# Another stored order of instructions and twenty warm-up matmuls instead of fourteen, in a one-core transformer block

## The chip, the core and the metric

The kernel runs on one core of a Trainium2 chip. A core has five engines that run their own instruction streams side by side: TensorE (PE in the profile; its weight loads are PEld), VectorE (DVE), ScalarE (ACT), GpSimd (POOL) and SyncE (SP, which here only starts transfers). They meet through semaphores. The metric is the device time of one execution in microseconds (us); lower is better.

## The reference

One sequence of 2048 positions with 448 features goes through two halves, each under adaptive layer norm. The six modulation vectors come from `mod = silu(c) @ w_mod`.

```python
h = layernorm(x) * (1 + ca) + sa
q, k, v = split(h @ wqkv)                 # 16 heads of 28
scores = q @ k.T * 28 ** -0.5             # masked: 0 <= i - j < 256
x = x + ga * (softmax(scores) @ v @ wo)
h = layernorm(x) * (1 + cb) + sb
z = gelu(h @ w_in)                        # 1792 wide, halves z1 and z2
g = w_sp @ layernorm(z2) + b_sp[:, None]  # w_sp is 2048 x 2048
x = x + gb * ((z1 * g) @ w_out)
```

Inputs and output are bf16.

## The kernel before

The sequence is cut into 16 tiles of 128 positions, in blocks of 1, 1, 2, 4, 4 and 4 tiles. For a block the kernel computes the statistics of x (st, L609; mv_all, L612), the reciprocal deviation (rs_all on POOL, L617), the normalised tile xn (L631 on DVE, L630 on POOL, or ScalarE), its transpose hT (by PE against an identity for the first three blocks, evacuated at L693 on ScalarE or L698 on VectorE; by transfers for the rest, modulated at L707), and then the projections to Q, K and V. Heads lie in groups of four; the weights of Q and K are therefore copied from the loaded wqk_raw into a padded layout WQK (L733 to L735, on DVE, ScalarE or POOL). The first tile's projections read wqk_raw itself where they can, four 32-column matmuls side by side (`mm_heads`, L779).

Attention goes by single tiles at first and then by pairs: scores into PSUM (28-row matmuls on QKT), exp on ScalarE into the tile arena (L887), causal and window masks on POOL (L890), products with V (32-column matmuls on Vaug), then on VectorE a 32x32 transpose oq out of PSUM (L1058), reciprocal (L1059), normalisation o_sb (L1063) and transpose back (L1067), and the projection wo with the residual added into x_sb (L1077). The second half computes z1 and z2 by blocks, and a last phase (from about 116 us on) multiplies w_sp, transposed by transfers, with the normalised z2 and projects out.

Nothing is scheduled while the kernel is built. Each step is recorded as a numbered operation with its dependencies and its choices of engine (`Planner.op`, L66), and a stored string `ORDER` (L179) names the operations in the order in which they are emitted: a number, behind a point the choice of engine, behind a slash the PSUM bank or buffer. `schedule` (L82) reads it; `emit` (L117) splits it into one in-order program for each engine and puts a semaphore wait ahead of an instruction where an operand, or the last user of its buffer, demands one:

```python
for tok in ORDER.split():
    head, _, picks = tok.partition("/")
    num, _, opt = head.partition(".")
    o = self.ops[int(num)]
```

So the string decides three things at once: what stands behind what on an engine, on which engine an operation with a choice runs, and which buffer's last reader it has to wait for. An engine never overtakes a waiting instruction. `column_tiles` (L106) then looks at PE's row: 128-row matmuls that stand between column-tiled ones are issued as four 32-column pieces as well (L464 instead of L467).

The first operations on PE are warm-ups: matmuls of a constant tile warm that nothing reads (loop at L1243). They stand in `ORDER` like everything else and can be put between waits.

Of the kernel before, what the change touches and what calls it, by code (L numbers as in the profile page):

```python
# [179 lines left out]
32 34 1 0 22 21 25 23 27 1693/0 1694 1695 1696 1697 1698 2 3 4 8 11 31 67 68 36 6 7 5 35 69 37/7 1699 12 24 28 26 70 71/4 9 10 20 13 15 18 14 74/6  # L180
72/2 33 38 39 40/1 41 42 43 44 45 46 47 76/7 48 49 50 78/4 51 52 53 54 55 56 73.1 125 126 75 79 1700 1701 127 90/6 95/1 85/0 62.2 63.2 1702 105/2 1703
96 86 91 80/4 106 81 180 128 129 130.1/1 77 57.1 60.1 61.1 65.1 64.1 87 97 182 92 82 88 98 83 93 84 99 94 181 89.1 183 66 58.2 59.2 184 185 115/3 116
117 107 118 108 119 109 131/7 132.1 245 249 133/4 134 1704 1705 496/0,0 498/1 150/0 1706 135/2 140/1 151 152 165/3 166 141 136 137 138 153 167 168 142
143 139 169 246 186 251 247 250 252 248 154 144 110/1 100/0 101 111 170/2 171 112 145/3 113 172 114 173 102 103 104 174.1 160/1 155/0 146 147 148 149
156 157 161 158 159 162 163 164 497/1,1 30.1 188.1/2 190/3 120/6 253 17 413 501/0 187.1/4 189 191.1 254 255 256/3 192/1 193 194 121 175/2 176 513/0,1
517/7 514/5 177 122 123 494/3 124.1 215/1 178 216 179 225/0 227 217 226 228 502 499 16 495 19 260 257.1/1 261 229 520/1,0 523/8 521/9 218.1 195/2
219.1 196 230/0 231 197 198 233 232 220/3 221 199.1 205/1 207 206 208 200/2 201 203 202 223 222 209 534/1,0 234.1 417 334 328 330 332 331 204 224
536/1 535/5 258.1/2 262 259.1/4 518 515 29 263 235/1 210/2 240/3 241 238.1 213.1 243.1 212 237 242 244.1 500/0 211 214.1 267 537/1,0 329 335 333 336
503 236 504/0 264.2 538 540 323/3 278/2 266.1 326 281 324 279 265.1 325 327 337 414 505 411 338 239.1 539 280 282 524/0 506/1 342/3 339/2 340/1 341/4
343 345 346 344 542/0,1 543/1 546/0 544/4 541 547/2 545 548 268/3 271 519 270 516 288/2 290 522 303/1 269 304 272 525/0 549/1,0 550/0 551/4 289 305  # L190
308/3 273/0 291.1 306.1 311.1 276.1 412 415 526 292.1 418 307.1 416 527/0 274 275 277 309 552/1,0 553 554 555 556 310 312.1 283/2 285 558/0 284 298/1
528/2 419 420 300 557 299 560 286.1 301.1 287 587/0,1 588/3 589/2 561 559 293/3 562 507/0 302.1 294 295 296 569/0 570 508/1 529/2 509 510 297 530 511
512 590/1,0 591 531 532 563/0 567 565 566 564 571.1/0 572/0 573/1 574 533 349 568 578/0 593 595/2,1 599/4 348.1 347.1 350 421 575 576 376/0 378 577
579 377 379 380.1 580/0 592 594 596/0 597/1 602/1,0 603/4 604/5 361/1 364 362 363 365.1 581/1 908 911 905 906 910 907 381/0 382 384 605/1,2 1426 606
383 385.1 608 366/1 367 368 369 370.1 614/0 611 610 640/1,0 642/0 641/1 598 600/2 613 422.2/3 936 938 582/1 583 584 585 586 937 942 607 318/3 320 609
601 356/2 357 358 396/1 612 615 622/0 623 943 399.1 359.1 321.1 360 643/1,0 646 398 319 397 322.1 922/0 923 924 925 926 400.1 927 928 929 930 644
648/2,0 649/3 313/1 315 314 619/0 316 652/2 617 620 655/1,2 657/2 939 940 941 944 616 317.1 621 618 423.1/0 425.1/1 424.1/2 624.1/0 647 645 625/1 913
912 426 909 428 631/0 656/4 351/1 352 354.1 353 406/2 409 371/3 386/0 658/1,0 661 632 633/0 374.1 389.1 388 634/0 355.1 407 408 410.1 635/1 636 387
390.1 945 659 372 637 638 639 693/0,1 373 375.1 653/4 650/1 651 654 662 668/0 666 667 664 663 660 665 946 675/0 401/1 404.1 427 429 431.2 430.1 432.1
695/5 694/3 676 947.1/0 433.1 696/1,2 697 698 403 402 626/0 405.1 627 628 629 630 701/0,1 677/0 454/1 457 674/0 456 455 458.1 672 671 673 669 670  # L200
684/0 961 962 678/0 699 705/0 700 953/2 706/1 707 702/2 703/4 708/1,2 709/1 710/0 391/1 393 392 449/0 450 452 451 453.1 685 686/1 711/1,0 712 713 714
715 394 395.1 687/1 464/3 467 679/0 680 466 681 682 444/2 465 468 446 746/0,1 447 445 683 918 1425 917 948 748/4 448.1 704 949/0 951/1 723/0 722 726
727 725 724 737/0 738 739.1/0 747/2 434/1 749/1,2 435 437 436 438.1 752 753 688/0 689 690 691 692 959 963 964 965 750 751 754/0,2 755/3 721/0 720 718
719 459/1 461 761/1,0 460 756/0 757 758/1 759/2 760 960 966 462 463.1 967 762/0 763/5 479/3 469/2 480 717 716 728/0 729 482.1 472.1 481 470 483
764/1,0 765 730/1 471 473.1 439/1 484/0 767 731/0 950 1428 952 954 921 1429 485 487 486 968 488.1 969 740/1 799/2,1 800/3 442.1 441 440 443.1 773/0
766 768 958.1 956.1 770 769 772 771 774 781/0 782 955 976.1/2 801/1 802/0,2 805 806 741/1 742 743 732/0 733 734 735 736 783/1 803 804 807/2,1 811/4
744 776/0 775 777 778 779 812/3 814/1,0 745 784/0 780 808/2 816/4 809/0 813 785/1 786 787 788 815/0 790/0 791 789 792/0 474/0 817/0,2 818 477 475 476
478.1 931/1 793/2 919 920 977 916 915 933 932 810 819 820 821 852/0,1 853/2 854/5 822/0 826 823 825 957.1 794/3 795 796 824 1035/2 1036 827 834/0 797
798 1037 935 934 986 835 988 982 984 983 989 985 987 1038 1043.1 855/0,1 856 858 970/1 974/2 972/0 857 859 1052/0 1054 1039/2 1040 1069/3 1071 1070
1053 1041 1072 1055 1042 1077.1 1060.1 1044.1 860/0,1 864/1 1090/1 1056/3 1091 828/0 832 830 831 489/2 829 833 1058 1057 1092 490 1435 914 1434 971  # L210
973 975 836.1/1 843/0 990 865/2 991 861/3 862/4 1059 492.1 1093 1061.1 867/1,0 869/0 868/4 1073/0 491 837/0 838/3 839 840 841 1095 493.1 844 845.1/0
980.2 1075 1086/1 1088 1087 842 1005 1076 1089 1094 846/1 992 981 978.1 997.1/1 979.1 999/2 870/2,0 873 998 1000 1431 995.1/0 866 863 874 871 872
1096/1 1295/7 1296 1305/6 1297 1307 1300/3 1150/0 1301 1154 1156 1074 1078 847/2 848 1151 849 1152 1330/1 1303 1298 1079/0 1299 1157 1153 1333 1308
850 851 1155 1306 876/0 878 1332 1302 1304 1103/2 1104 880 1331 1334 993/1 1335/7 875 879 1336 1107/1 877 1108 1340/1 1081 1007 1080 887/0 1006 1082
1008 888 1342 1105 1106 1110 1338 1343 1309 1158/2 1009 1160 1097 889.1/0 890/1 885/0 886 1124/0 882 1315/6 1109 1111.1 1112.1 883 1120 1337 881 884
896/0 1316 1122 1317 1339 1310/3 1320/7 1312 1341 1344 1325/0 1126 1322 1323 1318 1313 1328 1127 1123 1321 1121 996 994 1010 1011 1319 1012.1/2 891/3
1324 1014.1/1 1444 1436 1015 1013 1445 1430 1446 1449 892 1125 893 1128/3 897 1001.1 898.1/0 1003.2 899/0 894 900/0 1326 1370/6 1311 1180/0 1375/7 901
902 903 1184 1002.1 1004.1 1377 1186 1185 1181 1327 1159 1161 1162 895 1098 1099 1100 1163 1329 1314 904 1365/2 1290/1 1366 1368 1373 1378 1293 1183
1187 1022 1164 1023 1101 1102 1020 1021 1083 1024 1129 1025 1084 1026 1130 1029.1/2 1027.1/0 1030 1028 1433 1432 1457 1440 1437 1438 1452 1441 1453
1439 1443 1427 1442 1456 1451 1450 1376 1182 1292 1367 1371 1291 1372 1188/2 1190 1085 1189 1019.1 1369 1374 1294 1379 1285/0 1199/0 1286 1380/3 1200  # L220
1195 1201 1355/2 1197 1381 1357 1169/1 1165 1166 1171 1350/1 1196 1198 1202 1168 1383 1358 1353 1288 1172 1018.1 1191 1131 1045/1 1132 1133 1047 1192
1193 1046 1048 1049 1134 1050 1033.1 1034.1 1203/0 1205 1051 1351 1352 1016.2 1354 1287 1289 1210/0 1211 1170 1167 1382 1212 1356 1173/3 1214 1359
1174 1204 1194 1206 1207 1175 1176 1177 1360/1 1362 1345/0 1361 1229/1 1231 1225 1346 1217 1213 1017.2 1232 1348 1363 1228 1215 1226 1216 1031.2 1384
1364 1218/1 1390/3 1385/1 1230 1227 1233/2 1410/2 1392 1347 1391 1386 1255/0 1256 1259 1139/1 1135 1178 1179 1219 1220 1221 1208 1209 1222 1261 1349
1032.2 1257 1140 1142 1388 1393 1138 1262 1258 1062/3 1063 1223 1064 1234 1065 1224 1260 1387 1400/0 1394 1389 1141 1405/3 1402 1406 1407 1137 1401
# [72 lines left out]
def bass_adaLN_cond__sliding_block__mixer_gmlp__prompt_kernel(  # L298
# [809 lines left out]
    for bi, (T, z2s, z1s) in enumerate(BATCH):  # L1108
        gelus = []
        pr = T + 0.9  # L1110
        for zi, t in enumerate(z2s):
# [3 lines left out]
            def hst(c_, r, t=t):  # L1115
# [3 lines left out]
                           lambda c_, r, i=i: w_in_sb[r, c_, FH + i * D:FH + (i + 1) * D], D, joint=joint, idx=i, rprio=zp + 0.005) for i in range(2)]  # L1119
# [184 lines left out]
```

## Time and profile before

| | us |
|---|---|
| median of 3 runs | 268.02 (267.23 to 268.22) |
| profiled execution | 268.87 |
| its span | 267.1 |
| PE busy | 259.2 |
| VectorE busy | 167.2 |
| ScalarE busy | 128.3 |
| POOL busy | 96.6 |

How the rows are read: a timeline row has the start, the length, the engine, the line, the operation, what it writes and reads, partitions and sizes, how many instructions it joins, and in brackets the idle time ahead of it with what ended that time. A DVE, ACT or POOL instruction can overlap the next by a little. A row of stages has for each engine the busy time and, in brackets, the instructions in it. A releaser is put down by the semaphore event that was last by the profile, and "issue" means that the profile shows no semaphore for which the engine waited.

### The profile page before, as it was taken

What the parts mean: (1) busy time and instruction counts of PE and PEld (TensorE: products, weight loads), DVE (VectorE), ACT (ScalarE), POOL (GpSimd) and SP (SyncE); (2) the same over time, 40 slices, a digit from 0 to 9 for tenths busy, and PEclk for the clock granted to TensorE, in tenths of its full rate; (3) what the DMA queues carried; (4) which work ended last, traced back from release to release, by engine and by line L of the source; (5) the groups of instructions that cost most, each with busy time, mean ns of one, the idle gap of its engine ahead of it and who ended that gap; (6) DMA issues with size and microseconds to landing.
All of it is one profiled execution on the core that took longest, in us unless ns stands there. A gap on an engine that the chain in (4) does not pass through costs nothing.

```text
span 267.1 us, 7649 instructions
## 1 busy us (share of the span) xinstructions
PE 259.2 (97%) x3341; PEld 128.9 (48%) x3341; DVE 167.2 (63%) x388; ACT 128.3 (48%) x182; POOL 96.6 (36%) x148
## 2 busy tenths in 40 slices
PE   7999799999989999999999999999999999999996
PEld 3666345655445554544444444444444444444453
DVE  3899979978879899669988711306111814314455
ACT  4899879989989999866896300000000000000000
POOL 3784747878785888564422300000000000000000
PEclk9999999999999999999999999999999999999999
DMA  6963163574095590857799890000000000001023
GB/s 225 365 174 64 22 158 116 130 125 103 2 106 160 134 132 2 122 120 141 168 183 140 199 189 7 2 0 0 0 2 0 0 0 2 0 17 52 2 86 121
DMA packets 61022, 23.86 MB, mean 89 GB/s; under 512 B 49854, under 2 KB 60861, under 8 KB 60989
## 3 DMA queue, kind: packets, MB, share of 16 engines
q1 hardware_dynamic: 60715, 22.92, 40.5%
q8 instruction: 26, 0.43, 0.7%
q10 hardware_dynamic: 274, 0.46, 0.5%
q14 instruction: 7, 0.06, 0.1%
HBM read 9.47 MB, written 1.84 MB: 42 GB/s over the span
## 4 chain that ended last, share of the span: by engine, by line
PE 92%; DVE 3%; DMA 2%; issue 1%; ACT 0%; SPq 0%; DVEq 0%
PE ps L467 82%; PE ps L464 9%; DMA wmod_sb<-in_w_mod_dram 2%; DVE xn L631 1%; PE ps L779 1%; DVE oq L1058 1%; ACT arena L887 0%; DVE Vaug L837 0%; DVE hT L707 0%; DVE x_sb L1077 0%; DVE o_sb L1063 0%; DVE st_all L609 0%; DVE QKT L820 0%; SPq L498 0%; DVE mv_all L612 0%
## 5 line engine op out<-in xcount | busy, mean ns | idle before, releaser
L887 ACT ACTIVATE arena<-ps 128x1024 bf16<-128x1024 f32 x76 | 72.7, 1030 | 2.5 <-PE ps L467 2.3
L1212 DVE TENSOR_TENSOR tmpg<-ps,bsp_bc 128x512 bf16<-128x512 f32 x28 | 19.1, 688 | 63.6 <-PE ps L467 63.5
L467 PE MATMUL ps<-QKT,z 128*128 128x512 bf16 x224 | 50.1, 379 | 0.0
L890 POOL TENSOR_SCALAR_AFFINE_SELECT arena<-arena 128x512 f32<-128x512 f32 x60 | 40.4, 688 | 17.5 <-ACT arena L887 14.6
L467 PEld LDWEIGHTS ps<-QKT,z 128*128 128x128 bf16 x224 | 21.9, 98 | 26.4 <-ACT z1T L1154 0.3
L617 POOL TENSOR_TENSOR rs_all<-ve_all,neghalf 128x1 f32<-128x1 f32 (+2 forms) x27 | 18.7, 700 | 23.9 <-DVE ve_all L616 23.6
L467 PE MATMUL ps<-w_spD,z 128*128 128x512 bf16 x112 | 26.9, 379 | 0.0
L467 PE MATMUL ps<-w_spC,z 128*128 128x512 bf16 x112 | 26.8, 379 | 0.0
L467 PE MATMUL ps<-w_in_sb,hT 128*128 128x448 bf16 (+1 forms) x108 | 25.9, 354 | 0.0
L467 PE MATMUL ps<-hT,w_in_sb 128*128 128x512 bf16 (+1 forms) x94 | 24.3, 380 | 0.0
L467 PE MATMUL ps<-hT,WQK 128*128 128x128 bf16 (+3 forms) x127 | 21.9, 301 | 1.4 <-DVE mv_all L612 1.4
L467 PE MATMUL ps<-w_out_sb,z1T 128*128 128x448 bf16 (+2 forms) x119 | 22.3, 341 | 0.0
L609 DVE BATCH_NORM_STATS2 st_all<-z2raw 128x6 f32<-128x448 bf16 x32 | 18.9, 615 | 2.1 <-ACT z2raw L1135 1.6
L467 PE MATMUL ps<-arena,Vaug 128*32 128x128 bf16 x720 | 18.5, 221 | 1.3 <-issue 1.2
L609 DVE BATCH_NORM_STATS2 st_all<-x_sb 128x6 f32<-128x448 bf16 x32 | 18.7, 609 | 1.4 <-DMA x_sb<-in_A_x_dram 1.3
L467 PE MATMUL ps<-QKT 28*64 28x64 bf16 (+3 forms) x944 | 17.8, 210 | 0.8 <-issue 0.4
L467 PEld LDWEIGHTS ps<-arena,Vaug 128*32 128x32 bf16 x720 | 14.1, 95 | 8.4 <-issue 1.4
L1154 ACT ACTIVATE z1T<-ps 128x512 bf16<-128x512 f32 x28 | 15.8, 601 | 4.6 <-PE ps L467 2.9
L467 PEld LDWEIGHTS ps<-w_spD,z 128*128 128x128 bf16 x112 | 11.0, 98 | 13.1
L467 PEld LDWEIGHTS ps<-w_spC,z 128*128 128x128 bf16 x112 | 11.0, 98 | 13.1
L467 PEld LDWEIGHTS ps<-QKT 28*128 28x128 bf16 (+1 forms) x944 | 11.3, 98 | 12.2 <-ACT arena L887 7.9
L467 PEld LDWEIGHTS ps<-w_out_sb,z1T 128*128 128x128 bf16 x119 | 11.6, 98 | 10.2
(92 smaller groups left out, 340.5 us busy)
## 6 DMA issues: line engine op xcount, KB each, us to landing
wmod_sb<-in_w_mod_dram SPq DMA_DIRECT2D x8, 224.0 KB, 4.1
w_in_sb<-in_B_w_in_dram SPq DMA_DIRECT2D x8, 224.0 KB, 3.0
out_dram<-fin SPq DMA_DIRECT2D x16, 112.0 KB, 1.7
x_sb<-in_A_x_dram SPq DMA_DIRECT2D x3, 448.0 KB, 6.1
bsp_bc<-in_B_b_sp_dram SPq DMA_DIRECT2D x1, 512.0 KB, 5.3
wqk_raw<-in_A_wqkv_dram SPq DMA_DIRECT2D x1, 452.0 KB, 5.6
wmod_sb<-in_w_mod_dram SPq DMA_DIRECT2D x1, 448.0 KB, 4.3
wmod_sb<-in_w_mod_dram ACTq DMA_DIRECT2D x1, 448.0 KB, 4.8
```

Source lines behind the costliest of these rows:

```text
L464: last = e.matmul(out_[32 * j:32 * j + 32], lhsT=lhsT[:, 32 * j:32 * j + 32], rhs=rhs, start=st, stop=sp, tile_position=(0, 32 * j), **kw)
L467: return e.matmul(out_, lhsT=lhsT, rhs=rhs, start=st, stop=sp, **kw)
L609: st = [dve("%sst%d" % (name, i), prio, dve_ns(D), lambda e, i=i, s_=s_: e.bn_stats(st_all[:, slot, t, i, :], s_()), deps, tens) for i, s_ ...
L617: r = pool(name + "rs", prio, 420 + 148 * n, lambda e: e.tensor_tensor(rs_all[:, slot, t0:t1], ve_all[:, slot, t0:t1], neghalf[:, t0:t1], ...
L631: return e.tensor_scalar(dst, src, mv_all[:, slot, t, 0:1], rs_all[:, slot, t:t + 1], ALU.subtract, ALU.mult)
L779: last = e.matmul(out_[32 * j:32 * j + 32], lhsT=lhsT[j], rhs=rhs, start=st, stop=sp, tile_position=(0, 32 * j))
L887: return P.op(name, pr, [("act", 925, lambda e: e.activation(e_out(), e_in(), ACT.Exp, scale=SCALE))], [s_op, t_exp0], tens + [pt], table= ...
L890: return pool(name, pr, pool_ns(n), lambda e: e.affine_select(out=pt32(slot_out.slot, off, dims), in_=pt32(slot_in.slot, off, dims), patte ...
L1058: tq = dve("oq%d" % j, pr - 10, dve_ns(512), lambda e, pv_ten=pv_ten, qt=qt: e.transpose(out=oq[:, qt.slot, :], in_=ps[:, pv_ten.slot, :]) ...
L1154: g = P.op("z1g%d_%d" % (tb, ft), pr - 19, [("act", act_ns(512), lambda e: e.activation(z1T[:, ft, tb * 512:(tb + 1) * 512], ps[:, ten.slo ...
L1212: a = dve("ga%d_%d" % (tb, ft), pr, dve_ns(512), lambda e, tb=tb, ten=ten, tg=tg: e.tensor_tensor(tmpg[:, tg.slot, :], ps[:, ten.slot, :], ...
```

## The change

Two things change: the loop that records the warm-ups, and the string. All other code is the same, and so is what is computed.

```diff
-    for i in range(14):
-        n_ = 512 if i < 9 else 256
+    for i in range(20):
+        n_ = 512 if i < 10 else 256
```

All 59 lines of the string differ; the first of each is shown.

```diff
 ORDER = """
-32 34 1 0 22 21 25 23 27 1693/0 1694 1695 1696 1697 1698 2 3 4 8 11 31 67 68 36 6 7 5 35 69 37/7 1699 12 24 28 26 70 71/4 9 10 20 13 15 18 14 74/6
+21 1693/0 1694 1695 1696 0 32 35 34 15 1 2 3 4 8 6 7 11 27 22 25 36 37/0 1697 1698 1699 1700 1701 33 38 40/1 41 42 43 44 45 46 47 48 49 50 51 52 53 54
...
```

The new order uses other engines for 53 operations. Warm-ups apart, PE, ScalarE, VectorE and POOL do the same operations as before in sum: ScalarE has 181 instead of 179 of them, VectorE 390 instead of 386, POOL 138 instead of 144. PE has 3404 matmuls instead of 3341, since more of the 128-row ones are cut into column tiles, and 110 changes of the number of rows used by consecutive matmuls (128, 64 or 32) instead of 116.

The start of PE's row, before (c goes through one,crz; modulation through sc_sb,wmod_sb; transposes through ident,xn):

```order
L467 MATMUL ps<-warm 128x512 x6
L467 MATMUL ps<-one,crz 128x1 x4
L467 MATMUL ps<-warm 128x512
L467 MATMUL ps<-ident,xn 128x128 x2
L467 MATMUL ps<-sc_sb,wmod_sb 128x1 x16
L467 MATMUL ps<-ident,xn 128x128
L467 MATMUL ps<-sc_sb,wmod_sb 128x1 x6
L467 MATMUL ps<-ident,xn 128x128
L467 MATMUL ps<-sc_sb,wmod_sb 128x1 x10
L467 MATMUL ps<-warm 128x512 x2
L779 MATMUL ps<-hT,wqk_raw 32x128 x12
```

And now:

```order
L467 MATMUL ps<-warm 128x512 x4
L467 MATMUL ps<-one,crz 128x1 x4
L467 MATMUL ps<-warm 128x512 x5
L467 MATMUL ps<-sc_sb,wmod_sb 128x1 x32
L467 MATMUL ps<-ident,xn 128x128 x3
L467 MATMUL ps<-warm 128x512
L467 MATMUL ps<-ident,xn 128x128
L467 MATMUL ps<-warm 128x256 x7
L779 MATMUL ps<-hT,wqk_raw 32x128 x4
```

The products of c moved up by two warm-ups, the transposes of the first tile behind all of the modulation, and seven warm-ups of 256 columns stand ahead of the first projection where two of 512 stood.

The start of ScalarE's row, before:

```order
L564 ACTIVATE one<-one 128x1
L693 ACTIVATE hT<-ps,modT 128x128 x3
L734 ACTIVATE WQK<-wqk_raw 128x2x256
L734 ACTIVATE WQK<-wqk_raw 64x256 x3
L734 ACTIVATE WQK<-wqk_raw 128x2x256
L817 ACTIVATE QKT<-ps 128x128 x5
```

And now:

```order
L564 ACTIVATE one<-one 128x1
L734 ACTIVATE WQK<-wqk_raw 128x2x256
L693 ACTIVATE hT<-ps,modT 128x128 x3
L734 ACTIVATE WQK<-wqk_raw 64x256 x3
L734 ACTIVATE WQK<-wqk_raw 128x2x256
L817 ACTIVATE QKT<-ps 128x128 x5
```

One copy into WQK moved ahead of the three evacuations of the first tile's transposes. Which of the copies these are changed as well: one of the wide ones went from ScalarE to POOL and one came from POOL.

VectorE's row at about 27 to 33 us, between the first and the second tile's transpose oq, before:

```order
L1058 STREAM_TRANSPOSE oq<-ps 128x512
L612 BN_AGGR mv_all<-st_all 128x2
L1059 RECIPROCAL rec_all<-oq 128x16
L609 BN_STATS st_all<-x_sb 128x6
L647 SCALAR_TENSOR_TENSOR nm_all<-mv_all,rs_all 128x4
L837 CAST Vaug<-ps 128x16x28
L1063 TENSOR_TENSOR o_sb<-oq,rec_all 128x16x28
L631 TENSOR_SCALAR xn<-x_sb,mv_all,rs_all 128x512 x4
L1058 STREAM_TRANSPOSE oq<-ps 128x512
```

And now:

```order
L837 CAST Vaug<-ps 128x16x28
L647 SCALAR_TENSOR_TENSOR nm_all<-mv_all,rs_all 128x4
L1058 STREAM_TRANSPOSE oq<-ps 128x512
L1059 RECIPROCAL rec_all<-oq 128x16
L631 TENSOR_SCALAR xn<-x_sb,mv_all,rs_all 128x512 x2
L1063 TENSOR_TENSOR o_sb<-oq,rec_all 128x16x28
L609 BN_STATS st_all<-x_sb 128x6
L820 CAST QKT<-ps 128x512
L1058 STREAM_TRANSPOSE oq<-ps 128x512
```

Two of the four normalisations xn between the two transposes moved to POOL and ScalarE, the cast into Vaug stands ahead of the first transpose, and one cast into QKT (L820) has come between them.

The transfers that SP starts are the same, in another order: the two small pieces of wqk_raw come ahead of x's second tiles, one half of wv ahead of the other, x's last tiles in exchanged order, and one transposed block of w_sp instead of four is started before about 85 us. From the last block's transposes on, 30 transfers remain in both.

More of the change, by code (lines that the diff above doesn't have):

```diff
@@ L184 @@
[L184 to L187, printed above, removed]
@@ L236 @@
[L236 to L238 removed]
+21 1693/0 1694 1695 1696 0 32 35 34 15 1 2 3 4 8 6 7 11 27 22 25 36 37/0 1697 1698 1699 1700 1701 33 38 40/1 41 42 43 44 45 46 47 48 49 50 51 52 53 54
+55 67 68 26 24 23 69 28 70 71/2 31 76/0 74/3 72/7 56 125 77.1 126 61 127 1702 78/4 1703 1704 58.2 29 39 62.1 73 182 180 183 1705 1706 1707 1708 1709
@@ new lines @@
+574 595/2,0 599/0 575 576 376/0 378 379 377 596/4 602/1,0 603/5 579 577 580/0 380.1 581/0 361/1 364 363 362 365.1 381/0 384 382 605/1,2 604/4 936 383
+385.1 366/1 368 367 369 370.1 938 939 940 592 600/1 597/2 598 614/0 611 613 606 607 601 608 609 640/0,1 641/0 642/1 425.1/4 423.1/0 422.1/1 610
+424.2/2 582/1 583 612 318/3 584 585 356/2 357 358 319 586 942 937 615 622/0 623 624.1/0 359.1 321.1 643/1,0 646 647 396/1 399 320 397 322 905 906 910
+907 909 908 922/0 923 924 925 926 927 398 928 360.1 400.1 941 943 644 648/2,0 649/3 929 930 944 313/1 316 616/0 315 314 619 617 655/1,2 620 652/2
@@ new lines @@
+1590/1 1591 1461 1479 1480/3 1529 1530 1540/3 1574/7 1531 1668/2 1532/1 1454 1455 1481 1533 1551 1669 1670 1644/6 1645 1541 1542 1543 1646 1671 1575
+1462/0 1463 1647 1576 1577 1672/3 1648/2 1544/1 1545 1673 1578/1 1554 1488/6 1489 1555 1470/2 1482/3 1610/7 1471 1472 1473 1534/1 1535 1579 1556/3
+1580/5 1474/1 1605 1581 1582 1464/0 1606 1656/2 1611 1465 1490 1466 1657 1467 1658 1659 1483 1491 1557 1649 1660/2 1475 1468/1 1469 1536 1484 1607
+1522/2 1485 1523 1524 1583 1612 1613 1512/0 1525 1608/1 1661 1486/0 1537 1516/3 1487 1526/0 1527 1492/0 1493 1538/3 1584/0 1517 1592/2 1585 1518
@@ new lines @@
+1508/1 1593 1598/5 1599 1650/6 1600 1594 1595 1519 1596/0 1539 1614/2 1597 1615 1520/3 1513 1601 1651 1509 1652 1521 1602/2 1514/5 1570/7 1603 1653
+1654/0 1638/2 1639 1640 1558/6 1571 1559 1662/0 1663 1572/6 1560/3 1655 1609 1510/1 1616/5 1664 1500/7 1624/1 1625 1501 1504/6 1641 1505 1566/3 1506/0
+1515 1511 1573 1507 1567 1665 1617 1632/6 1633 1634 1568/7 1642/3 1643 1626/4 1502/0 1666/0 1627 1635 1636/2 1620/1 1621 1628/7 1637 1667 1622/1
+1618/5 1619 1623 1503 1569 1674/0 1682/5 1675 1676/2 1562/6 1683 1563 1629 1561 1684/4 1685 1630/0 1631 1564/6 1677 1565 1678/5 1679 1680/4 1681
@@ L239 @@
+1686/3 1687 1688/1 1689/6 1690 1691 1692
 """
```

98 lines of the change are left out of this document (44 added, 54 removed).

## The prediction

> **What bounds the kernel now.** The page's head and table of engines, read first, say which engine fills the span; the third line, from the table of DMA queues, is needed further down.
>
> ```profile
> span 267.1 us, 7649 instructions
> PE 259.2 (97%) x3341; PEld 128.9 (48%) x3341; DVE 167.2 (63%) x388; ACT 128.3 (48%) x182; POOL 96.6 (36%) x148
> ...
> q8 instruction: 26, 0.43, 0.7%
> ```
>
> TensorE is busy 97% of the span, so a new order can only win idle time of PE, or time that PE loses inside its busy stretches. The same engines by stage (busy us and count of PE, weight loads, DVE, ACT, POOL; clock; DMA share; GB/s):
>
> ```profile
> 0.00:13.00 13.00, 11.23 (x143) 5.90 (x144) 7.91 (x27) 8.71 (x21) 7.05 (x21) 1.00 0.89 293
> 13.00:36.00 23.00, 21.60 (x433) 12.69 (x434) 22.30 (x54) 21.06 (x37) 13.77 (x20) 1.00 0.39 92
> ...
> 60.00:80.00 20.00, 18.33 (x532) 9.87 (x530) 16.13 (x35) 18.37 (x21) 15.98 (x23) 1.00 0.50 72
> 80.00:95.00 15.00, 14.52 (x407) 7.86 (x406) 13.59 (x27) 13.85 (x16) 10.85 (x16) 1.00 0.62 158
> ...
> 150.00:250.00 100.00, 100.00 (x469) 45.78 (x468) 31.99 (x65) 0.00 (x0) 1.27 (x2) 1.00 0.11 26
> ```
>
> From 150 us on PE never waits, and the diff leaves this part's matmuls as they are. All that can move lies ahead of 95 us. The waits of PE (total, times, longest) name it:
>
> ```profile
> PE ps L467 <- issue: 1.6, 2, 1.2
> PE ps L467 <- POOL warm L537: 1.4, 1, 1.4
> PE ps L467 <- DVE mv_all L612: 1.4, 1, 1.4
> PE ps L467 <- ACT arena L887: 0.4, 1, 0.4
> ```
>
> So four things are to be priced: the start, the 1.4 us put down to mv_all, two waits of 1.6 us in which nothing released PE, and 0.4 us behind an exp. The sum is made against the profiled execution: 268.87 us, of which 267.1 are span. It stands 0.85 above the median of the runs, 268.02, so each term is taken off that median.
>
> **The start.** The timeline of the first 13 us, cut to what carries the argument:
>
> ```profile
> 1.41 2.74 PE L467 MATMUL ps<-warm 128*128 128x512 bf16 x6 [1.41 <-POOL warm L537]
> 6.73 1.01 PE L467 MATMUL ps<-warm 128*128 128x512 bf16 x2
> 7.11 1.16 ACT L693 ACTIVATE hT<-ps,modT 128x128 bf16<-128x128 f32 x3 [1.03 <-DVE modT L594]
> 7.35 1.17 POOL L735 COPY WQK<-wqk_raw 128x512 bf16<-128x512 bf16 x2 [2.71 <-DMA wqk_raw<-in_A_wqkv_dram]
> 7.71 0.51 PE L779 MATMUL ps<-hT,wqk_raw 128*32 128x128 bf16 x12
> 8.14 2.44 ACT L734 ACTIVATE WQK<-wqk_raw 128x512 bf16<-128x512 bf16 x5
> 8.79 0.62 PE L779 MATMUL ps<-hT,wqk_raw 128*32 128x128 bf16 x16
> 10.64 0.82 PE L467 MATMUL ps<-hT,WQK 128*128 128x128 bf16 x6
> 10.66 0.61 ACT L817 ACTIVATE QKT<-ps 128x128 bf16<-128x128 f32 x3
> 11.39 0.45 ACT L817 ACTIVATE QKT<-ps 128x128 bf16<-128x128 f32 x2
> 11.93 0.81 ACT L693 ACTIVATE hT<-ps,modT 128x128 bf16<-128x128 f32 x2
> 12.65 1.02 ACT L887 ACTIVATE arena<-ps 128x1024 bf16<-128x1024 f32 x1
> 12.79 2.45 PE L467 MATMUL ps<-hT,WQK 128*128 128x128 bf16 x39
> ```
>
> PE's dense run begins at 12.79, when ScalarE has evacuated the second block (row at 11.93), and the first exp stands right behind that evacuation, at 12.65. So ScalarE's chain from 7.11 to 12.65 sets the start: three evacuations, five copies, five QK evacuations, two evacuations. The new order keeps all fifteen pieces in number, but puts a copy from wqk_raw ahead of the first evacuation; that copy can begin when the load lands, at 7.35 by POOL's row, not at 7.11: +0.24. On the other side, the gaps between the rows (10.58 to 10.66, 11.27 to 11.39, 11.84 to 11.93: 0.29) are waits for PE, and five QK evacuations in one piece take 0.61 + 2 x 0.17 = 0.95 (0.17 is the step within the row of three), not 0.61 + 0.45 = 1.06: -0.11. If PE is early enough, that is +0.24 - 0.40 = -0.16; I take **-0.2**.
>
> Is PE early enough? Its first projection waits for the evacuation behind that copy: 0.6 us for the copy (POOL's two take 1.17; ScalarE's five mean 0.49) and 0.4 for one evacuation after 7.35 put it at about 8.4 to 8.6, against 7.71. Behind it stand 16 column-tiled projections of four matmuls and 8 whole ones up to the next transposes. At the pace of the rows (0.62 for four projections, 0.82 for six whole ones) that is 2.5 + 1.1 = 3.6 us, ending at 12.1: later than the 11.46 of before by 0.6, and the first exp with it. At the pace of the row at 12.79 (2.45 / 39 = 0.063 each) it is 0.9 to 1.6 us, and PE waits for ScalarE instead. So the six added warm-ups decide: they fill PE from the single-column products of the modulation to the first projection. With a late clock the start costs +0.6, with an early one -0.2; the lower bound is -0.4, should the load land 0.24 earlier as well. The rows say how late the clock was before: warm-ups of 512 columns took 0.46 at 1.41 and still 0.50 at 6.73, 5.3 us after PE began, and only the row at 12.79 is at double pace, though the view of stages gives 1.00 throughout. Before, PE had 1.77 us of idle time in those 13, and long stretches of products one column wide; the new order closes most holes ahead of 5.5 us, so I take the early rise, at 6 in 10.
>
> The Trainium skill, "TensorE: Matmul & The Clock Gate", Part 1, has the array start at half rate and go to full after about 3.4 us of sustained work, in a window that runs freely, so that the moment varies from run to run. By that rule PE, at work from 1.41, would have been at full pace by some 8.2 us in the kernel before (an estimate from that page); the row at 10.64 (0.82 over six, 0.137 each against 0.063 at 12.79) disagrees. The rule speaks against the change too, since it counts time and not warm-ups: by it the start is the -0.2 of above when the window falls well, and the +0.6 when it does not.
>
> **The wait at 31.3 us.** VectorE and PE there:
>
> ```profile
> 28.40 0.61 DVE L837 CAST Vaug<-ps 128x448 bf16<-128x448 f32 x1
> 29.47 2.82 DVE L631 TENSOR_SCALAR xn<-x_sb,mv_all,rs_all 128x512 bf16<-128x512 bf16 x4
> 32.21 0.70 DVE L1058 STREAM_TRANSPOSE oq<-ps 128x512 f32<-128x512 f32 x1
> 32.84 0.13 DVE L612 BATCH_NORM_AGGREGATE mv_all<-st_all 128x2 f32<-128x6 f32 x1
> ...
> 31.26 0.35 PE L467 MATMUL ps<-wv_sb,hT 128*128 128x448 bf16 x1
> 32.97 0.71 PE L467 MATMUL ps<-hT,WQK 128*128 128x512 bf16 x3 [1.36 <-DVE mv_all L612]
> ```
>
> PE stands from 31.6 to 32.97 for a bank that the transpose oq at 32.21 frees; mv_all, the page's name, only ended nearest. The transpose itself stood behind four normalisations, 2.82 us. In the new order two of the four have gone to POOL and ScalarE: -2 x 0.705 = -1.41. Between the two transposes oq there is a cast of 512 columns more (+0.61, by the cast of 448) and an aggregation less (-0.13). So oq ends 0.9 earlier and PE's wait shrinks from 1.36 to 0.45: **-0.9**. Bounds: -1.36, the whole wait; and 0, since VectorE is busy 22.30 of 23 us in this stage and whatever is pushed behind oq may be late next, namely the normalisations whose transposed tiles the projections after 36 us read. One of the two now hangs on ScalarE (21.06 of 23), the other on POOL (13.77), which has room.
>
> **Changes of form on PE.** Between matmuls that use 128, 64 or 32 rows PE loses a little:
>
> ```profile
> 16.04 0.73 PE L467 MATMUL ps<-wv_sb,hT 128*128 128x448 bf16 x3
> 16.70 0.40 PE L467 MATMUL ps<-QKT 28*128 28x128 bf16 x16
> 17.04 0.74 PE L467 MATMUL ps<-wv_sb,hT 128*128 128x448 bf16 x3
> 17.62 0.92 PE L467 MATMUL ps<-wmod_sb,sc_sb 128*128 128x448 bf16 x4
> ```
>
> Three matmuls of 448 columns take 0.66 to the start of the next when it is of another form, 0.58 when it is not: 0.08, say 0.1. The new order has 110 such changes where there were 116: **-0.6**, bounds -0.6 and 0. It also splits more 128-row matmuls into four column tiles (3404 instead of 3341 matmuls); the columns streamed are the same, so I put 0 on that.
>
> **ScalarE, 60 to 95 us.** Between blocks 4 and 8 the swaps give ScalarE about one operation more:
>
> ```profile
> 87.98 0.40 PE L467 MATMUL ps<-QKT 28*128 28x192 bf16 x16 [0.40 <-ACT arena L887]
> ```
>
> ScalarE is busy 18.37 of 20 and 13.85 of 15 us there, and PE waits for its exp at this place. One operation is 0.49 (a copy) to 1.02 (an exp); about 0.6, half of it in ScalarE's own holes: **+0.3**, bounds 0 and +0.6.
>
> **Late instructions.** The two waits without a releaser:
>
> ```profile
> 63.69 0.52 PE L467 MATMUL ps<-QKT 28*64 28x64 bf16 x42
> 64.61 0.29 PE L467 MATMUL ps<-QKT 28*64 28x64 bf16 x22 [0.40 <-issue]
> ...
> 79.61 0.33 PE L467 MATMUL ps<-arena,Vaug 128*32 128x128 bf16 x9 [1.19 <-issue]
> ```
>
> Both fall inside a run of small matmuls. The queue named instruction brought 26 packets, 0.43 MB in sum, 16.5 KB each; 2 x 3341 instructions of PE over 26 is 257 to a packet, so one packet holds some 128 matmuls with their weight loads. At 12 ns (0.52 over 42) these last 1.6 us. A packet's transfer is 0.7% of 16 x 267 us over 26, 1.15 us, to which its waiting behind other transfers is added. So PE runs dry where such a run empties a packet sooner than the next comes. The new order has the same runs of scores and value products at nearly the same density, and fewer early loads of w_sp beside them: **0**, bounds -1.59 (both gone) and +2.4 (two more of the longer kind). The Trainium skill, "Runtime: NRT & Kernel Launch", Instruction fetch mechanics, calls the crossing into a new 16 KiB block mostly hidden; by that sentence these waits would be nothing, and the rows' 0.40 and 1.19 show otherwise.
>
> **The sum.** -0.2 - 0.9 - 0.6 + 0.3 + 0 = -1.4: span 265.7, and from the median 268.02 - 1.4 = **266.6 us**. Measurement can tell about 0.5%, 1.34 us, from no change: faster is below 266.68, slower above 269.36. With the terms' bounds, an early clock and no change in the fetches, the forecast's own range is 265.7 (-0.4 - 1.36 - 0.6) to 268.4 (-0.2 + 0.6).
>
> **The rivals.** *No late instructions.* Were the two packets moved off the dense runs, 1.59 more would go: 266.6 - 1.6 = 265.0. For it: two places of 26, and small shifts of the packets' borders suffice. Against it: the matmuls there are as small as before.
>
> *The clock stays down through the start.* Then the start costs +0.6 instead of -0.2, and the forecast loses 0.8: 267.4, no change. For it: the slow row at 6.73; against it: PE is filled from 1.41 to 8.4 now.
>
> *Slower, by late instructions.* Place: the runs of scores and value products between 60 and 105 us, where four packets are as dense as those two. Price: 1.19 each, 4.8 in all against the 1.6 of now, +3.2: 266.6 + 3.2 = 269.8. It decides when four packets of 1.6 us, not two, meet a transfer that takes 1.6 + 1.19 = 2.8 us with its waiting; three give 268.6, no change yet. For it: DMA shares of 0.50 and 0.62, PE that waits less elsewhere and so runs into the packet's end sooner, and 63 matmuls more, half a packet. Against it: fewer loads at that place.
>
> **How the numbers follow.** Forecast 0.45, just under the bound, so 0.25 of it faster and 0.20 the same; no late instructions 0.18, faster; clock down 0.17, the same; late instructions 0.20, slower. Faster 0.43, same 0.37, slower 0.20. The range reaches from 264.4, a little under the first rival, to 269.6, which leaves out about half of the last: 264.4 to 269.6.
>
> **What would show it.** In the profile after: the first exp at about 12.45 and a row of dense projections from 12.6 on, with 256-column warm-ups at double pace before 9 us; oq around 31.9 behind two xn, and PE's wait there under 0.6; two waits on issue of 1.6 together; the exp's wait at 88 up to 0.7; nothing from 150 us on but the same chain, earlier by the sum. The prediction is wrong if another wait of PE over 1 us appears between 36 and 95 us, if waits on issue come three times or more, or if the first exp is later than 12.65.

## The result

The changed kernel takes 266.31 us (264.75 to 267.52, 13 runs) against 267.86 for the kernel before in the same sittings: ratio 0.9944, 95% interval 0.9919 to 0.9968, that is 1.5 us less with 0.9 to 2.2 as the interval. In a later sitting it was 266.0 us, ratio 0.9953 (0.9932 to 0.9973). The profiled execution took 266.55 us with a span of 264.8; against the profile before the span is 2.3 us shorter, against the medians 1.5. That gap is a subject below; the profiled execution of before, 268.87, also lies above all 13 of the timed ones (268.36 at most).

The page after, its head, its engines and the queue of instructions:

```profile
span 264.8 us, 7787 instructions
PE 257.9 (97%) x3404; PEld 129.4 (49%) x3404; DVE 165.9 (63%) x392; ACT 129.1 (49%) x184; POOL 90.5 (34%) x142
...
q8 instruction: 26, 0.43, 0.7%
```

The waits of PE, and the stages as before (columns as in the prediction):

```profile
PE ps L467 <- POOL one L538: 1.4, 1, 1.4
PE ps L464 <- ACT hT L710: 1.2, 1, 1.2
PE ps L467 <- issue: 0.5, 1, 0.5
PE ps L467 <- DVE crz L560: 0.3, 1, 0.3
PE ps L467 <- ACT arena L887: 0.2, 1, 0.2
PE ps L467 <- DVE oq L1058: 0.2, 1, 0.2
```

```profile
0.00:13.00 13.00, 11.01 (x154) 5.93 (x155) 7.91 (x28) 8.67 (x21) 6.38 (x21) 1.00 0.89 288
13.00:36.00 23.00, 21.77 (x447) 13.29 (x444) 21.29 (x56) 21.45 (x36) 15.40 (x22) 1.00 0.66 102
...
60.00:80.00 20.00, 19.98 (x553) 10.66 (x548) 17.63 (x37) 19.08 (x23) 16.29 (x24) 1.00 0.54 126
80.00:95.00 15.00, 14.33 (x423) 7.91 (x430) 14.15 (x27) 14.56 (x18) 11.19 (x17) 1.00 0.58 84
```

The wait of 1.4 behind mv_all is gone, a wait of 1.2 behind a modulation on ScalarE (hT, L710) is new, and the two waits on issue of 1.6 have become one of 0.5. From 13 to 36 us PE is busy 21.77 us, hardly more than the 21.60 of before: one wait replaced the other. The places in the timeline:

```profile
7.61 0.99 PE L467 MATMUL ps<-warm 128*128 128x256 bf16 x7
12.34 1.02 ACT L887 ACTIVATE arena<-ps 128x1024 bf16<-128x1024 f32 x1
12.36 2.57 PE L467 MATMUL ps<-hT,WQK 128*128 128x128 bf16 x40
26.17 0.56 PE L464 MATMUL ps<-wv_sb,hT 128*32 128x448 bf16 x8 [1.23 <-ACT hT L710]
28.27 0.65 DVE L631 TENSOR_SCALAR xn<-x_sb,mv_all,rs_all 128x512 bf16<-128x512 bf16 x2
30.96 0.72 DVE L1058 STREAM_TRANSPOSE oq<-ps 128x512 f32<-128x512 f32 x1 [0.19 <-PE ps L467]
53.64 0.24 PE L467 MATMUL ps<-arena,Vaug 128*32 128x128 bf16 x3 [0.47 <-issue]
82.92 0.93 PE L467 MATMUL ps<-wo_sb,oT 128*128 128x448 bf16 x4 [0.20 <-DVE oq L1058]
85.63 0.40 PE L467 MATMUL ps<-QKT 28*128 28x192 bf16 x16 [0.23 <-ACT arena L887]
```

and the last rows of PE in the chain that ended last, of before and of after:

```profile
116.29 148.29 PE ps L467 x729
```

```profile
114.03 148.23 PE ps L467 x723
```

PE ends at 264.58 and at 262.26: 2.32 us earlier in the profiled execution. By place, against the terms of the prediction:

| place | before | after | difference | predicted |
|---|---|---|---|---|
| start of PE's dense run | 12.79 | 12.36 | -0.43 | -0.2 |
| wait near 26 us | 0 | 1.23 | +1.23 | not seen |
| wait near 31 us | 1.36 | 0 | -1.36 | -0.9 |
| waits on issue | 0.40 + 1.19 | 0.47 | -1.12 | 0 |
| ScalarE, then VectorE, 80 to 90 us | 0.40 | 0.23 + 0.20 | +0.03 | +0.3 |
| the rest: changes of form, small gaps | | | -0.67 | -0.6 |
| sum | 264.58 | 262.26 | -2.32 | -1.4 |

### The profile page after: what moved, and what is told of

Its sections match the earlier page's. It is cut to its first block, busy times and chain, and to the rows that moved or that the text cites. A ratio compares the mean times of both kernels' runs of the same rounds, so it can differ in the third digit from the quotient of the medians.

```text
span 264.8 us, 7787 instructions
## 1 busy us (share of the span) xinstructions
PE 257.9 (97%) x3404; PEld 129.4 (49%) x3404; DVE 165.9 (63%) x392; ACT 129.1 (49%) x184; POOL 90.5 (34%) x142
## 4 chain that ended last, share of the span: by engine, by line
PE 90%; ACT 5%; DMA 2%; POOL 1%; SPq 1%; issue 1%; DVE 0%; ACTq 0%
PE ps L467 78%; PE ps L464 12%; ACT arena L887 4%; DMA hT<-xn 1%; ACT hT L693 1%; DMA crow<-in_c_dram 1%; PE ps L779 1%; SPq L717 1%; POOL arena L890 0%; ACT hT L710 0%; POOL xn L630 0%; DVE wo_sb L523 0%; DVE fin L1234 0%; ACT QKT L817 0%; DVE crz L559 0%
## 5 line engine op out<-in xcount | busy, mean ns | idle before, releaser
L467 PE MATMUL ps<-QKT,z 128*128 128x512 bf16 x224 | 51.1, 379 | 0.0
L890 POOL TENSOR_SCALAR_AFFINE_SELECT arena<-arena 128x512 f32<-128x512 f32 x60 | 39.0, 669 | 15.9 <-ACT arena L887 12.8
L467 PE MATMUL ps<-w_out_sb,z1T 128*128 128x448 bf16 (+2 forms) x119 | 23.0, 341 | 0.0
L467 PE MATMUL ps<-hT,WQK 128*128 128x128 bf16 (+4 forms) x123 | 19.4, 290 | 0.1
L630 POOL TENSOR_SCALAR xn<-x_sb,rs_all,nm_all 128x512 bf16<-128x512 bf16 x21 | 16.4, 787 | 6.6 <-DVE nm_all L621 2.0
L467 PE MATMUL ps<-arena,Vaug 128*32 128x128 bf16 x720 | 17.9, 221 | 0.5 <-issue 0.5
L1234 DVE TENSOR_TENSOR fin<-ps,x_sb 128x448 bf16<-128x448 f32 (+2 forms) x17 | 9.8, 594 | 13.6 <-PE ps L467 13.4
```

The source lines that it names most:

```text
L467: return e.matmul(out_, lhsT=lhsT, rhs=rhs, start=st, stop=sp, **kw)
L630: return e.tensor_scalar(dst, src, rs_all[:, slot, t:t + 1], nm_all[:, slot, t:t + 1], ALU.mult, ALU.add)
L890: return pool(name, pr, pool_ns(n), lambda e: e.affine_select(out=pt32(slot_out.slot, off, dims), in_=pt32(slot_in.slot, off, dims), patte ...
L1234: fs.append(dve("fin%s%d" % (nm, t), pr, dve_ns(c1 - c0), lambda e, t=t, ten=ten, ft_=ft_, c0=c0, c1=c1: e.tensor_tensor(fin[:, ft_.slot, ...
```

## The experiments

A word on reading their profiles: in several of them 20 or 22 matmul records are missing (x3382 where the program has 3404). In those of the new order and its edits, six waits on issue of 0.16, and two of 0.28 and 0.16 put down to a reciprocal, stand at the same matmuls in each and not in the complete profiles. They are taken for such holes, as are those of 0.16 in the one such profile of the order of before, and are left out of what follows. All ratios are to the kernel before on the same chip.

### The six warm-ups alone, and the new order without them

```diff
-    for i in range(14):
+    for i in range(20):
...
-1700 1701 127 90/6
+1700 1701 1707 1708 1709 1710 1711 1712 127 90/6
```

> The order of before with the six added warm-ups alone: six matmuls of 256 columns right ahead of the first projection. Theory A (the clock follows how long PE is kept at work): PE is at double pace before 9.5 us, the first tile's projections end by 10.8 instead of 11.46, the dense run begins near 12.5 instead of 12.79, and the time is 0.3 below before. Theory B (the start of after is gained by the moved copies and casts, and the clock rises when it rises): six warm-ups at half pace cost 1.3 us, the projections end after 11.46, the dense run begins at 13.0 or later, and the time is 0.3 or more above before. Behind 13 us nothing changes but the borders of the instruction packets, by 12 instructions.

Measured: 268.01 us, ratio 1.0007 (0.9983 to 1.0030). In its profile the first exp is at 12.96, 0.31 later than before, though PE was at double pace earlier: six whole projections (last row) take 0.51 where they took 0.82. The first projections begin 1.33 later, behind the longer row of warm-ups.

```profile
6.81 2.29 PE L467 MATMUL ps<-warm 128*128 128x512 bf16 x8
9.04 0.51 PE L779 MATMUL ps<-hT,wqk_raw 128*32 128x128 bf16 x12
10.12 0.56 PE L779 MATMUL ps<-hT,wqk_raw 128*32 128x128 bf16 x16
11.39 0.51 PE L467 MATMUL ps<-hT,WQK 128*128 128x128 bf16 x6
```

In the profile these are the signs of theory B: the projections end at 11.90 and the dense run begins at 13.18. The time, 0.2 above before with an interval from 0.5 below to 0.8 above, decides nothing. Nor is the earlier double pace shown to come from the six warm-ups. Three other edits of the order of before, told below, keep its fourteen and have the same row at 0.51; here is the one with the four normalisations moved ahead:

```profile
10.90 0.51 PE L467 MATMUL ps<-hT,WQK 128*128 128x128 bf16 x6
```

The other side, the new order with the six taken out:

```diff
-    for i in range(20):
+    for i in range(14):
...
-1706 1707 1708 1709 85/0 1710
+1706 85/0
```

(and 1711 and 1712 taken out further on)

> The order of after without the six added warm-ups (three ahead of the first projection, one behind it, two around the first scores). Theory A: the clock rises as late as before, at about 12 us, the first exp comes at 12.8 to 13.0 instead of 12.34, and the time is 0.5 above after, 1.0 below before. Theory B: the first exp stays at 12.3 to 12.4 and the time is that of after, 1.5 below before.

Measured: 265.99 us, ratio 0.9926 (0.9898 to 0.9953): no slower than the new order with them. The profile shows the late clock that theory A expects (six whole projections still took 0.82 at 11.74), and an even later first exp, 13.72 instead of 12.34. (A kernel below that keeps all twenty had it at 14.18, so a late clock need not come from their absence.) And yet the span, 265.1, is only 0.3 longer, because PE's wait near 26 us shrank from 1.23 to 0.62 and no packet of instructions came late. In the profiles of the new order and of the edits made to it further down, the first exp lies between 12.34 and 14.18, and the 38th exp between 60.22 and 61.51, with little relation to it: what the start gains or loses, mostly does not arrive. Neither theory is right as it was put: the pace of PE moves the start, and the end hardly follows.

The same seven warm-ups, in kernels whose orders are alike up to there, show that the clock is not the order's alone. They took 0.99 in the new order, and in the last repeat of an edited one (told below):

```profile
8.39 1.70 PE L467 MATMUL ps<-warm 128*128 128x256 bf16 x7
```

The Trainium skill, "TensorE: Matmul & The Clock Gate", Part 1, says that the window which decides the clock runs freely and that the moment varies from run to run; these rows agree, while its 3.4 us of work were not enough here (PE was at work from 1.4 us in both).

### The normalisations ahead of the transpose oq

Two of them moved off VectorE, in the order of before:

```diff
-342/3 339/2 340/1 341/4
+342/3 339/2 340.1/1 341.2/4
```

> The order of before with one thing of the new one: two of the four normalisations ahead of the second transpose oq go to POOL and to ScalarE. Theory A: PE's wait at 31.3 us falls from 1.36 to 0.45 or less, nothing takes its place, and the time is 0.9 to 1.3 below before. Theory B: VectorE is the limit of that stage, or the normalised tiles come too late on ScalarE and POOL, so that another wait of about 1 us appears between 33 and 45 us and the time is that of before within 0.3.

Measured: 266.94 us, ratio 0.9967 (0.9948 to 0.9985), 0.9 below before (0.4 to 1.4): theory A in the time, and the size of the term, but not by its route. The wait behind oq is gone altogether, and half of it came back at once behind an exp that ScalarE's new normalisation delays.

```profile
30.62 0.70 DVE L1058 STREAM_TRANSPOSE oq<-ps 128x512 f32<-128x512 f32 x1
31.43 0.40 PE L467 MATMUL ps<-QKT 28*128 28x192 bf16 x16 [0.67 <-ACT arena L887]
```

The opposite edit, on the new order: both back on VectorE.

```diff
-339/4 342/1
+339/4 342/1 340/2 341/0
...
-340.1/2
...
-341.2/0
```

> The order of after with one thing undone: the two normalisations that went to POOL and ScalarE stand on VectorE again, ahead of the second transpose oq. Theory A: oq ends 1.4 later, a wait of PE of 0.7 to 1.4 comes back near 32 us, and the time is 0.7 to 1.0 above after, 0.6 below before. Theory B (the gain of after has other causes): no such wait, or one that is made up by 45 us, and the time is that of after within 0.3.

Measured: 265.13 us, ratio 0.9915 (0.9884 to 0.9946). Theory A fell: nothing got slower and no wait came back. The reason stands in one row. Four normalisations took 1.30 us here, and had taken 2.82 in the kernel before:

```profile
28.64 1.30 DVE L631 TENSOR_SCALAR xn<-x_sb,mv_all,rs_all 128x512 bf16<-128x512 bf16 x4
```

In the kernel before, POOL's masks ran all that time, one every 0.66 us, and each normalisation took one such turn. Here POOL rests until they are over (its idle time ahead of the masks stands in brackets):

```profile
29.52 3.29 POOL L890 TENSOR_SCALAR_AFFINE_SELECT arena<-arena 128x512 f32<-128x512 f32 x5 [1.04 <-ACT arena L887]
```

```profile
29.94 2.89 POOL L890 TENSOR_SCALAR_AFFINE_SELECT arena<-arena 128x512 f32<-128x512 f32 x4 [2.33 <-ACT arena L887]
```

The first of these rows is of before, the second of this kernel. The Trainium skill, "SBUF — State Buffer", "SBUF: two separate sides", calls the port pair that VectorE and GpSimd share "an exclusive lock, not a bandwidth split", held for a whole instruction; 0.33 alone and 0.70 beside masks of 0.66 agree with that.

To test it without any change of engines, the four were moved ahead inside VectorE's row of the kernel before, into POOL's pause:

```diff
-338 239.1 539 280 282 524/0 506/1 342/3 339/2 340/1 341/4
+338 342/3 339/2 340/1 341/4 239.1 539 280 282 524/0 506/1
```

> The order of before with one move inside VectorE's row: the four normalisations stand ahead of the cast into Vaug and of o_sb instead of behind them, where POOL has a mask at 27.8 to 28.5 and then nothing until 29.5; no engine, no other row changes. Theory A (the four took 2.82 in before, because POOL's masks ran beside them at 29.52 to 32.8, and 1.30 in the order of after with POOL idle): they take 1.3 to 1.9, oq ends 0.9 to 1.5 earlier, PE's wait of 1.36 falls under 0.4, and the time is 0.9 to 1.3 below before. Theory B (a normalisation costs 0.7 here and only their number ahead of oq counts): they take 2.8 again, oq ends where it did, the wait and the time are those of before.

Measured: 267.04 us, ratio 0.9987 (0.9967 to 1.0008). In the profile theory A holds to the letter:

```profile
28.40 1.39 DVE L631 TENSOR_SCALAR xn<-x_sb,mv_all,rs_all 128x512 bf16<-128x512 bf16 x4
30.38 0.83 PE L464 MATMUL ps<-hT,WQK 128*32 128x512 bf16 x12 [0.34 <-DVE Vaug L837]
30.96 0.72 DVE L1058 STREAM_TRANSPOSE oq<-ps 128x512 f32<-128x512 f32 x1
```

The four take 1.39 instead of 2.82 and oq starts 1.25 earlier, so PE's wait behind oq goes, and 0.34 of it returns behind the cast that was moved back. Up to 37 us this profile is 0.87 ahead of the one before. In the time, though, the gain is not clear of zero: its interval reaches from 0.9 below before to 0.2 above. The profile does not show where it went: a wait on issue of 0.37 at 53 us is new, but the waits on issue sum to 1.64 against 1.59, and PE still ends 0.7 earlier than in the profile of before.

### The load ahead of the transposes

PE's new wait at 26.17 ends when the transposes of block 3 have landed and been modulated. SP starts four of them, in the kernel before and after:

```profile
18.01 5.24 SPq L717 DMA_TRANSPOSE hT<-xn  x4
```

```profile
17.14 6.75 SPq L717 DMA_TRANSPOSE hT<-xn  x4
```

They begin 0.87 earlier and take 1.51 longer, all of it in the second one, whose start lasts 2.78 instead of 1.3:

```profile
18.49 2.78 SPq L717 DMA_TRANSPOSE hT<-xn  x1
```

One suspect was the load of x's last four tiles, which stands right ahead of them and, in the new order, is later:

```diff
-20 260
+260
...
-263
+263 20
...
-413
...
-239.1
+239.1 413
```

> The order of after, with the load of x's last four tiles started behind the four transposes of block 3 instead of ahead of them, and the one statistic that reads it early moved behind the cast of the third tile's V. Theory A (PE's new wait of 1.23 at 26.17 us comes from transposes that stand in the transfer queues behind that load): the second transpose's start takes 1.3 us instead of 2.8, the last lands 1.2 or more earlier, PE's wait there falls under 0.4, and the time is 0.6 to 1.0 below after, that is 2.1 to 2.5 below before. Theory B (the transposes are late through what stands ahead of them on POOL and through the start of the first): the wait stays above 0.9 and the time is that of after, 1.5 below before.

Measured: 265.39 us, ratio 0.9932 (0.9912 to 0.9953). PE's wait there is 0.52, and the four starts take 6.05, with the first now at 2.12. So the load is not what lengthens them, or not alone: theory A is wrong in its mechanism. Theory B, which expected the wait to stay above 0.9, is not right either; PE came there at 26.79 instead of 24.94, for the clock rose late in that execution (six whole projections still took 0.80 at 12.41), and the data were ready at 27.31, later than the 26.17 of the new order. Over all profiles the four starts took 5.24 to 5.95 us in the five kernels with the order of before, and 5.74 to 6.75 in the nine with the new one. What adds the 0.5 to 1.5 us stays open. In the first profile of the new order a packet of instructions of another queue was fetched during the slow start, at 19.20, and in the order of before only after the four. But two kernels with the order of before had a start of 1.77 and of 1.99 as well, without that packet, and in the repeat of the new order the start of 1.99 was over before it came.

The wait near 26 us is not the new order's alone. In the order of before with cut warm-ups (told below), where the four starts took 5.95, PE waited 0.51 there, and its wait behind oq (put down to mv_all) was 0.70 instead of 1.36:

```profile
PE ps L467 <- DVE mv_all L612: 0.7, 1, 0.7
PE ps L464 <- ACT hT L710: 0.5, 1, 0.5
```

So it seems that what PE waits near 26 us it need not wait again at 31.

Both edits together:

> The order of after with two edits tried singly: the four normalisations on VectorE, and the load of x's last four tiles behind block 3's transposes. Theory A (each took something off): waits of PE at 26 and 32 us under 0.4 each, the time 0.2 to 0.6 below either alone, 2.6 to 3.0 below before. Theory B (their gains over after are scatter between executions): the time is that of after, 1.3 to 1.7 below before.

(The two edits above, in one kernel.) Measured: 267.14 us, ratio 0.9993 (0.9967 to 1.0020). It was the slowest of the four. A wait of 0.82 behind a cast on VectorE appeared at 32.18; the four normalisations ahead of it took 1.65, and POOL's masks began at 29.07, in their midst:

```profile
28.36 1.65 DVE L631 TENSOR_SCALAR xn<-x_sb,mv_all,rs_all 128x512 bf16<-128x512 bf16 x4
32.18 0.36 PE L467 MATMUL ps<-wv_sb,hT 128*128 128x448 bf16 x1 [0.82 <-DVE QKT L820]
```

Two gains of 0.6 and 0.9 over the new order made a loss together, which speaks for their having been scatter. But theory B's number did not come either: the time is only 0.4 below before, and 1.1 above the new order in the same sitting. The wait does not explain that, since the profiled execution that shows it, 266.23, was the fastest of the twelve. Why the two edits together cost so much stays open. The second timing of the order with four normalisations on VectorE also speaks for scatter:

> The new order with the four normalisations on VectorE, again, since its first timing lay below after on six executions only. Theory A (with POOL idle beside them the four cost 1.3, and ScalarE and POOL lose two operations, so that undoing this part of the change helps): 2.2 to 2.8 below before once more, and 0.8 or more below after. Theory B (scatter between executions): 1.3 to 1.7 below before, the time of after.

Measured: 265.58 us, ratio 0.9942 (0.9912 to 0.9972), the ratio of the new order itself. The new order repeated:

> The changed kernel again, unaltered, beside the two others on one chip. If what its first profile showed is a property of the order: PE at double pace before 9 us, one start of a transpose of block 3 of over 2 us, a wait of PE near 26 us of 0.9 to 1.3, none at 31 us, waits on issue under 0.6 in sum, and 1.3 to 1.8 below before. If it is scatter: the moment of the clock, the wait near 26 us or the waits on issue differ by more than 0.5 from the first profile, at the same median.

Measured: 266.0 us, ratio 0.9953 (0.9932 to 0.9973), with PE's wait near 26 us at 0.77 instead of 1.23, a slow start of a transpose (1.99 at first), none near 31 us, and 0.2 on issue. So the disappearance at 31 us and the wait at 26 us belong to the order; the size of the latter doesn't, nor does the gain at the start: the first exp is at 12.66 here, as late as before.

### Borders of the instruction packets

Both orders with the warm-ups cut into matmuls of 64 columns; the same columns, more instructions:

```diff
-mm(e, ps[:, w_ten.slot, 0:n_], warm[:, 0:128], warm[:, 0:n_], True, True)
+[mm(e, ps[:, w_ten.slot, q:q + 64], warm[:, 0:128], warm[:, q:q + 64], True, True) for q in range(0, n_, 64)][-1]
```

> The order of before with each warm-up cut into matmuls of 64 columns: the same columns, but 78 matmuls and so 156 instructions more ahead of all others, which moves the borders of the instruction packets by 156 of 256. Theory A (a wait on issue comes where a border falls into a dense run): the waits of 0.40 at 64 us and 1.19 at 78 us go or move to other places, and the time changes by up to 1.6 either way. Theory B (the dense runs themselves cause them): both stay where they are, 1.6 in sum, and the time is that of before.

Measured, in the order of before: 268.0 us, ratio 1.0017 (0.9994 to 1.0041). The waits at 64 and 78 us are gone and one of 0.35 stands at 55.7 us:

```profile
55.74 0.21 PE L467 MATMUL ps<-QKT 28*128 28x64 bf16 x3 [0.35 <-issue]
```

So the border decides where PE runs dry (theory A). But the time did not follow. The profiled execution ended 1.33 earlier than that of before, the timed ones did not; a single profile does not price these waits.

> The order of after with each warm-up cut into matmuls of 64 columns: 100 matmuls, 200 instructions more ahead of the rest, which moves the borders of the instruction packets by 200 of 256. Theory A (waits on issue in the profiled execution hang on where the borders fall, and weigh little in the other executions): the one wait of 0.47 at 53.6 us goes, waits at other places may come, the time stays within 0.5 of after. Theory B (the borders of after are a part of its gain): the waits on issue grow to 1 us or more and the time with them, to 0.5 to 0.8 below before.

Measured, in the new order: 268.6 us, ratio 1.0033 (1.0011 to 1.0056): all of the gain lost, and more. Its profile has waits on issue of 0.40, 0.44, 0.24 and 0.66 at 20, 42, 55 and 65 us, 1.7 in sum against 0.47; the last of them:

```profile
65.10 0.25 PE L467 MATMUL ps<-QKT 28*64 28x64 bf16 x10 [0.66 <-issue]
```

That is 2.3 to 2.6 above the new order. Theory B, that the borders of the new order are a part of its gain, fits the time better, but the loss is larger than it expected, and the span of the profile is only 1.2 longer than that of the new order. The rest of the loss is in no profile. The cut warm-ups also changed the start, though the first exp, at 12.68, is only 0.34 later, and only this one shift of the borders was tried.

The profiles of all the kernels tell the same of the waits on issue, behind 15 us and without the holes. In the five with the order of before they come to 1.59, 1.16, 1.28, 1.64 and 0.35, the last with cut warm-ups. In the eight of the new order and its other edits they come to 0.47 at most.

### What a change of form costs

```diff
+    for i in range(3):
+        def fn(e, i=i):
+            for q in range(24):
+                r = 128 if i == 0 or (i == 2 and q % 2 == 0) else 32
+                last = mm(e, ps[:, f_ten.slot, 0:128], w_out_sb[0:r, 0, 0:128], w_out_sb[0:r, 0, 0:128], True, True, **({"tile_position": (0, 0)} if r == 32 else {}))
+            return last
```

> The order of after with 72 matmuls of 128 columns added at PE's very end, behind the last product, from w_out into a free bank: 24 of 128 rows, 24 of 32 rows, and 24 that alternate between the two. Nothing waits for them. Theory A (a change of the rows in use costs about 0.1 us): the first and second group go at 0.055 each, the third at about 0.17. Theory B (what the rows before showed came from other differences): all three go at 0.055 to 0.065. The time itself says nothing here, since the added work is at the end.

Measured, in one execution: theory A. Matmuls of 128 or of 32 rows among themselves go at 0.056 us, alternating ones at 0.160: 0.104 for each change. First the start of the 128-row group, then a stretch of the alternating one:

```profile
262.49 1.12 PE L467 MATMUL ps<-w_out_sb 128*128 128x128 bf16 x17 [1.36 <-DVE fin L1234]
...
265.85 3.33 PE L467 MATMUL ps<-w_out_sb 32*128 32x128 bf16 x20
```

(17 in 1.12 and 20 in 3.33 us; the last matmul of a stretch counts until its end.) Six changes fewer are 0.6 us at this price; what they cost in the kernel itself was not measured. It agrees with one sum. From the dense run to its last matmul, waits taken out, PE took 248.3 to 248.4 us in the four complete profiles with the order of before, and 247.8 in the two with the new one.

## Why the prediction was right, and where it was not

The time, 266.31, lies 0.3 from the forecast of 266.6, and the sign and the range held. The sum was right with terms that were not, and that it came so close is in part luck: +1.23 us near 26 us and -1.12 of late instructions, neither of them in the sum, nearly cancel in the profile.

**The start**: predicted -0.2, -0.43 in the first profile and -0.11 in the repeat, and it was priced against the wrong thing. Whether the clock rose early was left open rightly, but the step that failed is the one that carried the start's gain to the end of the kernel. Leaving the six warm-ups out cost nothing, and adding them alone gave nothing that the times show. What PE gains there it waits for at 26 us, for transposes that have not landed. The rival with the late clock was thus too dear. In three profiles with a late clock (first exp at 13.71 to 14.18) PE still ended at 261.9 to 262.5, against 262.26.

**The wait at 31 us**: predicted -0.9, and the edit alone measured -0.9, by another route: there the whole 1.36 went, and 0.67 came back behind an exp. In the new order the whole 1.36 went too. The step "-2 x 0.705" failed in its price: 0.705 was not what a normalisation costs but what it costs beside POOL's masks. Alone it costs 0.33, and so the new order gained by placing the normalisations where POOL rests, as well as by moving two of them away; with all four back on VectorE they still took 1.30. Against this stands +1.23 at 26 us, a wait that was in no term and in no rival. It stands ahead of 31 us, so part of the 1.36 may only have moved there; no run separates the two.

**Changes of form**: -0.6 predicted; 0.104 each was measured, 0.6 for six, and -0.67 is left over in the table. The price was right; that the remainder is all theirs is not shown.

**ScalarE**: +0.3 predicted, +0.03 found at this place. The wait for ScalarE itself fell, from 0.40 to 0.23, which was below the term's bounds; a wait of 0.20 for VectorE came beside it.

**Late instructions**: 0 predicted, -1.12 in the profiled execution. The argument that the runs are as dense as before was true and did not decide; the border's place did, as the first rival put it, and the other profiles of the new order show few such waits again. In the timed executions this term can't be read. Cutting the old order's warm-ups took 1.24 of such waits out of the profile and nothing out of the time, cutting the new order's added 1.27 to the profile and 2.3 to 2.6 to the time. Part of the difference between 2.3 us in the profiles and 1.5 in the medians is likely here, but that is argued, not shown.

## What to carry to other kernels

Before pricing an operation by its row, look at what its neighbour on the shared port did in the same microsecond: the same VectorE instruction was 0.33 or 0.70 us here, and in the profiles moving it by 1 us in its row brought about as much as moving it to another engine (in the times only the latter is clear of zero). A gain at the start is worth what the next external arrival lets through, so find the next wait for a transfer before adding it to a sum. And on a PE-bound kernel of small matmuls, repeat an experiment with 150 to 200 harmless instructions ahead of it. Here that moved the time of the new order by more than the whole change and that of the old one by nothing, and the place of the packet borders is the part of it that the profiles show.

## What was not expected of the hardware

The starts of DMA transposes on SP, 1.3 us each as a rule, lasted up to 2.78 without any semaphore. The clock's rise, with the same seven warm-ups of 256 columns, came by the first of them or after the last (0.93 to 0.99 against 1.70 us), while the row of stages shows a granted clock of 1.00 from the start in both.
